# Pooled attention and a SiLU layer: a third unit in the first product, key and value sums on Pool, x sums a tile ahead

## Chip, cores and metric

The kernel runs on one core of a Trainium2 chip. Its time is the device time of one execution in microseconds; a figure for a kernel is the median of several runs. The profile names the engines: PE (TensorE: matmuls; PEld is its weight load), DVE (VectorE), ACT (ScalarE), POOL (GpSimd, which also issues the casting and adding loads) and SP (SyncE, which issues stores).

## What is computed

There are 8 batches, 8 heads, 576 queries and a head size of 64. Keys and values are averaged over groups of 8 positions, so that each query meets 72 of them. The attention result is x, 4608 tokens by 512, and goes through two matrix products with a SiLU between them.

```
k_p = k.reshape(B, H, Sp, pool, D).mean(axis=3)
v_p = v.reshape(B, H, Sp, pool, D).mean(axis=3)
attn = softmax(scale * q @ k_p^T)
x = (attn @ v_p), rearranged to 4608 x 512
h = x @ w_in              # 512 x 2048
g = h * sigmoid(h)
out = g @ w_out           # 2048 x 512
```

## The kernel before

**Tiles.** Tokens are taken 512 at a time: nine tiles, t = 0 to 8 (loop at line 801). Each tile has a first product (`up`, line 467) that fills h_T, 16 groups of 128 hidden columns, and a second one (`down_quarters`, line 639) that makes 512 output rows. The attention of batch a = t + 1 is spread over tile t. Call U the start of a tile's first product and D the start of its second.

**Order of work.** The order on each engine is written by hand. `spread` (line 413) runs beside the matmuls of a product: each matmul of a plain group, and each pair of matmuls of a unit, is a step, and each filler, a function with a step number, is issued when its step is reached. A step number therefore places work in the queue of its engine, nothing more: an engine that isn't held by a wait (Pool above all) runs ahead of PE. Fillers in `f_up` belong to the first product, those in `f_down` to the second.

**First product.** A plain group (line 534) is four matmuls of 512 columns into one PSUM bank of the tag mm (three banks), then a SiLU on ACT. A unit (lines 424 to 523) treats four groups and two halves of the tokens as a 2 x 2 block product and does it by seven products instead of eight, each of four matmuls of 256 columns. Two of its accumulators, P and Q, lie in banks of the tag at (five banks, shared with the attention), R in one of mm. ACT copies P into r_sb (line 501); DVE makes rr_sb, t_sb and two c_sb from PSUM and r_sb (lines 504, 507, 516, 519); ACT then makes SiLU from two PSUM banks and two c_sb (line 492). Units take sums of x (`unit_x_sum`, line 449, five per tile, common to all units) and sums of weights (`unit_weight_sum`, line 442, five per unit). Tiles 2 to 6 have two units (groups 4 to 11) and eight plain groups. Tiles 7 and 8 have three units, called B, C and A (groups 4 to 7, 8 to 11 and 12 to 15), and four plain groups, in an order written in `THREE` (line 794), where A2 is product 2 of unit A.

**Second product.** It uses the same seven-product scheme: 112 matmuls of 256 columns, with sums of h_T (`hidden_sum`, line 609) that DVE makes late in the first product and early in the second. PE first reads the sums 2 and 5 for hidden groups 4 to 7 of each half. The last add of a tile (line 687) empties bank Q.

**Attention.** Queries come through POOL (`load_q`, line 134, two buffers) and are transposed on DVE in four parts (`q_transpose`, line 155). Keys of batches 3 to 7 come in two loads: `load_one` (line 176) writes the first half, `load_rest` (line 182) adds the second half to it in place and so must wait until the first has landed. Then DVE adds twice: `add_halves` (line 188, 72 x 1024 fp32) and `add_rest` (line 193, 72 x 512). For keys the result is kp, one buffer, which `k_transpose` (line 213) takes through PE and ACT to kz; for values it is vp, two buffers. The raw buffers k_raw and v_raw exist once, so a new load waits until the adds on the old data are done. Then follow, in three visits per batch, scores and exponentials (line 339), denominators (359) and numerators (378), which write x (xT).

Of the kernel before, what the change touches and what calls it, by code (L numbers as in the profile page):

```python
# [29 lines left out]
BF16 = mybir.dt.bfloat16  # L30
# [6 lines left out]
def kernel(  # L37
# [9 lines left out]
    nc = tc.nc  # L47

    B, H, S, D = q.shape
    POOL = 8  # L50
    SP = S // POOL
# [75 lines left out]
    batches = {}  # L127
# [57 lines left out]
            accum_op=ALU.add,  # L185
        )

    def add_halves(raw):
        nc.vector.tensor_add(
            out=raw[:, :, : 2 * D], in0=raw[:, :, : 2 * D], in1=raw[:, :, 2 * D :]  # L190
        )

    def add_rest(dst, raw):
        nc.vector.tensor_add(
            out=dst,
            in0=raw[:, :, :D], in1=raw[:, :, D : 2 * D],
        )

    def pool_k(b, stage):
        st = batches[b]  # L200
        raw = st["k_raw"]
        if stage == 0:
            add_halves(raw)
            return
        add_rest(kp[:SP], raw)

    def pool_v(b):
        st = batches[b]
        st["vp"] = mid.tile([SP, H, D], BF16, tag="vp", name="vp")
        add_halves(st["v_raw"])  # L210
        add_rest(st["vp"], st["v_raw"])

    def k_transpose(b, parts=(0, 1)):
        st = batches[b]
# [586 lines left out]
    for t in range(NT):  # L801
        a = t + 1
        f_up, f_down = [], []
        if t == 0:
            GA = 11
            items = [(g, 0, HS) for g in range(GA)]
            items += [(g, HS, NTT - HS) for g in range(GA)]
            items += [(g, 0, NTT) for g in range(GA, KG)]
            f_up += [(1, lambda: denominators(0, part(0, 1), on_dve=True))]
            f_up += [(5, lambda: denominators(0, part(1, 1), on_dve=True))]  # L810
            f_up += [(13, lambda: numerators(0, part(0, 1)))]
            f_up += [(17, lambda: numerators(0, part(1, 1)))]
        else:
            G = lambda *gs: [(g, 0, NTT) for g in gs]
            if t == 1:
                items = (
                    G(12, 13, 14, 15) + [(0, "251")] + G(8) + [(0, "43")] + G(9)
                    + [(0, "7h6")] + G(10) + [(0, "s")] + G(11, 0, 1, 2, 3)
                )
            elif t >= B - 1:  # L820
                items = []
                for it in THREE[t - B + 1].split():
                    items += [(("BCA".index(it[0])), it[1])] if it[0] in "ABC" else G(int(it[1]))
            else:
                items = (
                    G(12, 13) + [(0, "251")] + G(14) + [(0, "43")] + G(15) + [(0, "76")]
                    + [(1, "2")] + [(0, "hs")] + [(1, "51")] + G(0) + [(1, "43")] + G(1)
                    + [(1, "7h6")] + G(2) + [(1, "s")] + G(3)
                )
            if t < B - 1:  # L830
                for n in U_X:
                    f_up.append((0, lambda n=n: unit_x_sum(t, n)))
            for n in (2, 5):
                h_at = {B - 1: 54, B: 50}.get(t, 36 if t > 1 else 45)
                f_up.append((h_at, lambda n=n: hidden_sum(n, 4, 8)))
            f_up.append((56, lambda: hidden_sum(6, 4, 8)))
            for n, k0 in ((2, 0), (5, 0), (1, 4), (1, 0)):
                f_up.append((64, lambda n=n, k0=k0: hidden_sum(n, k0, k0 + 4)))
            f_down.append((33, lambda: hidden_sum(7, 0, 8)))
            f_down.append((71 if t < B else 50, lambda: hidden_sum(6, 0, 4)))  # L840

        for n, t0, f_to, at, parts in (
            (1, 0, f_down, 48, (0, PW)), (3, 0, f_down, 52, (0, PW)),
            (4, 1, f_up, 38, (0, PW)), (7, 1, f_up, 42, (0, PW)),
            (6, 1, f_up, 60, (0, PW)),
        ):
            for i in range(*parts):
                if t == t0:
                    f_to.append((at + i, lambda n=n, i=i: weight_sum(n, i)))
        if a < B:  # L850
            q_at = [15, 16, 17, 8] if t > 1 else [24, 25, 26, 2] if t else [82, 84, 86, 88]
            if t == 0:
                for j in range(2):
                    f_up.append((44 + 8 * j, lambda j=j: slot_sums("k", j)))
                    f_up.append((72 + 8 * j, lambda j=j: select_k(1, j)))
                    f_up.append((72 + 8 * j, lambda j=j: copy_k(1, j)))
                    f_down.append((20 + 10 * j, lambda j=j: slot_sums("v", j)))
                    f_down.append((37 + 3 * j, lambda j=j: select_v(1, j, "at")))
                    f_down.append((37 + 3 * j, lambda j=j: copy_v(1, j)))
            elif t == 1:  # L860
                for j in range(2):
                    f_up.append((0, lambda j=j: slot_sums("k", j, halves=True)))
                    f_up.append((22, lambda j=j: select_k(2, j)))
                    f_up.append((23, lambda j=j: copy_k(2, j)))
                    f_down.append((8, lambda j=j: slot_sums("v", j, halves=True)))
                    f_down.append((40, lambda j=j: select_v(2, j, "at")))
                    f_down.append((41, lambda j=j: copy_v(2, j)))
            else:
                f_up.append((22, lambda: k_transpose(a)))
                f_down.append((10, lambda: pool_v(a)))  # L870
            for n in range(4):
                f_to = f_down if t and n == 3 else f_up
                f_to.append((q_at[n], lambda n=n: q_transpose(a, n % 2, n // 2)))
            if t == 0:
                f_down.append((0, lambda: load_half_2("k", 0)))
                f_down.append((0, lambda: load_q(2)))
                f_down.append((0, lambda: load_half_2("k", 1)))
                for half in range(2):
                    f_down.append((31, lambda half=half: load_half_2("v", half)))
                for y in range(2):  # L880
                    for n in U_W:
                        f_down.append((6, lambda y=y, n=n: unit_weight_sum(y, n)))
            elif a + 1 < B:
                for stage in range(2):
                    f_down.append((73 + 8 * stage, lambda stage=stage: pool_k(a + 1, stage)))
                f_up.append((0, lambda: load_one(a + 1, "k")))
                f_up.append((48 if a + 1 == B - 1 else 1, lambda: load_q(a + 1)))
                f_up.append((2, lambda: load_rest(a + 1, "k")))
                f_down.append((11, lambda: load_one(a + 1, "v")))
                f_down.append((12, lambda: load_rest(a + 1, "v")))  # L890
            f_down.append((0, attn_tables))

            if t:
                sc_at, den_at, nu_at = (1, 31, 75), (31, 56, 97), (56, 97, 101)
            else:
                sc_at, den_at, nu_at = (1, 16, 30), (16, 30, 44), (44, 55, 56)
            for n, sg in enumerate(visits):
                f_down.append((den_at[n], lambda sg=sg: denominators(a, sg)))
                f_down.append((sc_at[n], lambda sg=sg: scores(a, sg)))

            for n, sg in enumerate(visits):
                if n < 2 or not 0 < t < B - 2:
                    f_down.append((nu_at[n], lambda sg=sg: numerators(a, sg)))
                if n == 0 and 1 < t < B - 1:
                    f_down.append((nu_at[n], lambda: numerators(a - 1, visits[2])))
        if t in (B - 2, B - 1):
            for n in (4, 1, 3, 7, 6):
                f_down.append((98 if t < B - 1 else 44, lambda n=n: unit_x_sum(t + 1, n)))
        if t == B - 2:
            k_w = big.tile([128, 4, 2, 256], BF16, tag="k_raw2", name="w_sum12")  # L910
            v_w = big.tile([128, 4, 2, 256], BF16, tag="v_raw2", name="w_sum12")
            w_sum1.append([k_w[:, i] for i in range(4)] + [v_w[:, 0]])
            for i, n in enumerate(U_W):
                f_down.append((73 if i < 2 else 81, lambda n=n: unit_weight_sum(2, n)))
        moe_tables()
        up(t, f_up, items)
        if t == 0:
            down(t, f_down, [(0, 1, 2), (3,)])
        else:
            down_quarters(t, f_down, last=t == NT - 1)  # L920
# [28 lines left out]
```

The softmax here doesn't subtract the row's maximum and nothing guards it: scores larger than these inputs give would overflow.

## Time and profile before

| | |
|---|---|
| median of 4 runs | 283.62 us (283.2 to 283.7) |
| profiled execution | 283.7 us |
| its span | 281.6 us |
| PE busy | 276.1 us |
| DVE busy | 223.2 us |
| ACT busy | 184.9 us |
| POOL busy | 61.1 us |
| first product, tiles 3 to 6 | 13.14, 13.16, 13.20, 13.10 us |
| second product, tiles 3 to 5 | 15.98, 16.00, 16.00 us |
| first product, tile 7 (three units) | 12.62 us |

The span goes from the first instruction to the last; the execution's own time has 2.1 us more around it. Rows of groups give a line of the kernel, the engine and operation, out<-in, the count, then busy time and the mean duration of one in ns, then the idle time before them and what ended it. Rows of a timeline give start and duration in us; neighbouring instructions of a kind are merged, and the end of one may lie past the start of the next. Rows of stretches give start and end, length, and the busy time of each engine. In these tables the tiles' products are cut at their first matmuls.

### The profile page before, as it was taken

How to read it: one execution, taken by the hardware profiler on the slowest of the kernel's cores; microseconds unless marked ns; L12 is line 12 of the kernel's file. 1: busy time of each engine (PE TensorE's matmuls, PEld its weight loads, DVE VectorE, ACT ScalarE, POOL GpSimd, SP SyncE). 2: the span in 40 equal slices, each digit the busy share in tenths (PEclk: the TensorE clock that was granted, in tenths of full speed). 3: DMA queues.
4: the chain of work that ended last, by engine and by line, in shares of the span. 5: the costliest groups of instructions: out<-in, count | busy, mean ns of one | idle time of the engine just before them, and what ended most of it. 6: DMA issues, size and time to landing. Idle time of an engine off the chain costs nothing.

```text
span 281.6 us, 6986 instructions
## 1 busy us (share of the span) xinstructions
PE 276.1 (98%) x2823; PEld 198.0 (70%) x2823; DVE 223.2 (79%) x413; ACT 184.9 (66%) x361; POOL 61.1 (22%) x79
## 2 busy tenths in 40 slices
PE   8989999999999999999999999999999999999995
PEld 4348544456777677767888876687767878788784
DVE  4787736889977798779877996898878898966983
ACT  1677766568577876687668857794779568426800
POOL 8565216232140214021402130442200000000001
PEclk9999999999999999999999999999999999999999
DMA  7999999896759853985497539499750032004004
GB/s 210 277 256 236 209 312 178 224 187 123 144 74 211 153 121 51 196 188 123 69 197 168 107 80 173 106 153 133 115 120 1 2 84 67 2 6 127 20 4 147
DMA packets 31312, 37.70 MB, mean 134 GB/s; under 512 B 10352, under 2 KB 22256, under 8 KB 31280
## 3 DMA queue, kind: packets, MB, share of 16 engines
q0 software_dynamic: 23920, 27.03, 52.7%
q1 hardware_dynamic: 6928, 9.58, 12.5%
q10 hardware_dynamic: 432, 0.66, 0.7%
q8 instruction: 22, 0.36, 0.5%
q14 instruction: 10, 0.08, 0.1%
HBM read 36.70 MB, written 9.44 MB: 164 GB/s over the span
## 4 chain that ended last, share of the span: by engine, by line
PE 91%; DMA 3%; DVE 3%; POOL 1%; issue 1%; DVEq 0%; POOLq 0%
PE hp_ps L544 24%; PE o_psP L652 15%; PE o_psQ L652 15%; PE u_psQ L484 8%; PE u_psP L484 8%; PE o_psR L652 5%; PE sc_ps L347 4%; PE o_ps L579 3%; DMA raw<-in_v_dram 3%; PE nu_ps L391 3%; PE u_psR L484 3%; PE den_ps L365 2%; DVE xT L400 1%; DVE w_sum L630 1%; POOL q_bf L132 1%
## 5 line engine op out<-in xcount | busy, mean ns | idle before, releaser
L544 PE MATMUL hp_ps<-xT,w_in_sb 128*128 128x512 bf16 (+3 forms) x380 | 74.5, 337 | 0.1
L652 PEld LDWEIGHTS <-h_sum 128*128 128x128 bf16 x640 | 60.6, 98 | 11.9 <-issue 1.3
L550 ACT ACTIVATE h_T<-hp_ps 128x512 bf16<-128x512 f32 (+2 forms) x87 | 46.4, 541 | 18.2 <-PE hp_ps L544 16.0
L612 DVE TENSOR_TENSOR h_sum<-h_T 128x1024 bf16<-128x1024 bf16 (+1 forms) x72 | 50.5, 744 | 5.0 <-ACT h_T L550 5.0
L544 PEld LDWEIGHTS <-w_in_sb 128*128 128x128 bf16 x380 | 36.2, 98 | 21.8 <-issue 0.6
L355 ACT ACTIVATE es<-sc_ps 72x384 bf16<-72x384 f32 (+1 forms) x100 | 39.0, 469 | 9.7 <-PE sc_ps L347 9.6
L484 PEld LDWEIGHTS <-w_sum 128*128 128x128 bf16 x340 | 33.3, 98 | 7.5
L652 PEld LDWEIGHTS <-h_T 128*128 128x128 bf16 x256 | 24.1, 98 | 4.5 <-issue 0.9
L400 DVE TENSOR_TENSOR xT<-nu_ps,rec 128x384 bf16<-128x384 f32 (+1 forms) x50 | 24.0, 534 | 2.0 <-PE nu_ps L391 1.8
L374 ACT ACTIVATE lnd<-den_ps 128x384 f32<-128x384 f32 (+1 forms) x23 | 11.1, 484 | 19.6 <-PE den_ps L365 19.6
L492 ACT ACTIVATE h_T<-c_sb 128x512 bf16<-128x512 f32 x34 | 20.7, 626 | 4.4 <-DVE c_sb L516 4.2
L270 DVE TENSOR_TENSOR raw<-raw 128x384 f32<-128x384 f32 (+3 forms) x20 | 12.4, 619 | 9.7 <-DMA raw<-in_v_dram 6.9
L516 DVE TENSOR_TENSOR c_sb<-u_psP,t_sb 128x512 f32<-128x512 f32 x17 | 11.7, 690 | 8.4 <-ACT kz L224 4.2
L183 POOL DMA_DIRECT2D raw<-in_k_dram x5 | 7.1, 1429 | 50.7 <-DMA raw<-in_k_dram 50.7
L556 POOL DMA_DIRECT2D out_dram<-o_sb x2 | 1.2, 592 | 77.0 <-issue 76.2
L652 PE MATMUL o_psP<-w_out_sb,h_sum 128*128 128x256 bf16 x128 | 17.6, 273 | 0.0
L501 ACT COPY r_sb<-u_psP 128x512 f32<-128x512 f32 x17 | 9.9, 584 | 10.3 <-PE u_psP L484 9.0
L652 PE MATMUL o_psQ<-w_sum,h_sum 128*128 128x256 bf16 x128 | 16.7, 273 | 0.0
L652 PE MATMUL o_psQ<-w_out_sb,h_sum 128*128 128x256 bf16 x128 | 16.6, 273 | 0.0
L652 PE MATMUL o_psQ<-w_sum,h_T 128*128 128x256 bf16 x128 | 16.5, 273 | 0.0
L652 PE MATMUL o_psP<-w_sum,h_T 128*128 128x256 bf16 x128 | 16.5, 273 | 0.0
L504 DVE TENSOR_TENSOR rr_sb<-u_psQ,r_sb 128x512 f32<-128x512 f32 x17 | 11.8, 691 | 5.6 <-ACT r_sb L501 5.0
(83 smaller groups left out, 466.9 us busy)
## 6 DMA issues: line engine op xcount, KB each, us to landing
out_dram<-o_sb SPq DMA_DIRECT2D x128, 64.0 KB, 4.6
raw<-in_k_dram POOLq DMA_DIRECT2D x10, 576.0 KB, 9.7
raw<-in_v_dram POOLq DMA_DIRECT2D x10, 576.0 KB, 7.9
q_bf<-in_q_dram POOLq DMA_DIRECT2D x6, 576.0 KB, 12.9
w_in_sb<-in_moe_w_in_dram POOLq DMA_DIRECT2D x8, 256.0 KB, 8.4
w_out_sb<-in_moe_w_out_dram POOLq DMA_DIRECT2D x4, 512.0 KB, 13.7
raw<-in_v_dram POOLq DMA_DIRECT2D x2, 768.0 KB, 11.3
raw<-in_k_dram POOLq DMA_DIRECT2D x1, 768.0 KB, 9.5
```

The lines of the kernel that those rows point to most:

```text
L270: nc.vector.tensor_add(out=raw[..., :w], in0=raw[..., :w], in1=raw[..., w : 2 * w])
L347: nc.tensor.matmul(sc[s][:, cs], lhsT=kz[b % 2][rows, g, c, :], rhs=st["qT"][rows, g, i0:i1, :, c], start=(c == 0), stop=(c == 1),)
L355: nc.scalar.activation(es[:, s, :], sc[s], func=AF.Exp, scale=score_scale)
L400: nc.vector.tensor_mul(out=xT[:, 2 * g0 + c : 2 * (g0 + ng - 1) + c + 1 : 2, cols], in0=nu[c][:, :w].rearrange("r (g n) -> r g n", g=ng), ...
L484: nc.tensor.matmul(ps[y, bank][:, u, :], lhsT=w[:, kk, 128 * u : 128 * (u + 1)], rhs=x[:, kk, :], start=first and u == 0 and kk == 0, stop ...
L492: nc.scalar.activation(h_T[:, g : g + 2, j * NQ : (j + 1) * NQ], src, func=AF.Silu)
L504: tt(out=rr_sb, in0=ps[y, "Q"], in1=r_sb, op=ALU.add)
L516: tt(out=c_sb[0], in0=ps[y, "P"], in1=t_sb, op=ALU.add)
L544: nc.tensor.matmul(hp_ps[:, r0:r1], lhsT=w_in_sb[:, kk, g * 128 : (g + 1) * 128], rhs=xT[:, kk, x0 : x0 + r1 - r0], start=(kk == 0), stop= ...
L550: nc.scalar.activation(h_T[:, g, n0 : n0 + n], hp_ps[:, :n], func=AF.Silu)
L612: nc.vector.tensor_tensor(out=h_sum[n][:, ks, :], in0=quarter(*a, ks), in1=quarter(*b, ks), op=op)
L652: nc.tensor.matmul(ps[b][:, c, :], lhsT=left(n, kt, c), rhs=W_OUT[n][:, kt, :], start=b not in begun, stop=kt == k1 - 1, skip_group_check= ...
```

## The change

1. Tiles 3 to 6 get the third unit too: the plain groups 12 to 15 become unit A, in the order of `THREE`.
2. The adds on raw keys and values of batches 3 to 7 go from DVE to POOL (`pool_rows`). The value adds of batch a are issued at step 2 of the first product of tile a - 1, in POOL's queue behind the first key load and the query load of batch a + 1 and ahead of the second key load; the key adds of batch a + 1 at step 13 of the second product, ahead of the second value load. From tile 2 on the first value load is issued in the first product. For batch 7 the query load comes later, behind the first value load.
3. The five sums of x for tiles 3 to 6 are issued at step 98 of the second product of the tile before, not at the start of their own tile.
4. The weight sums of unit A are made in tile 1 instead of tile 6.
5. From tile 3 on, the key transpose is issued at the head of the first product instead of step 22, two of the four query transposes at steps 4 and 14 of the first product and two at steps 4 and 8 of the second (before: three and one), and the first sums of h at step 54 instead of 36.

```diff
-    def add_halves(raw):
-        nc.vector.tensor_add(
+    def pool_rows(dst, raw):
+        nc.gpsimd.tensor_add(
             out=raw[:, :, : 2 * D], in0=raw[:, :, : 2 * D], in1=raw[:, :, 2 * D :]
         )
...
+        nc.gpsimd.tensor_add(out=dst, in0=raw[:, :, :D], in1=raw[:, :, D : 2 * D])
+
+    def pool_k(b):
+        pool_rows(kp[:SP], batches[b]["k_raw"])
 
     def pool_v(b):
         st = batches[b]
         st["vp"] = mid.tile([SP, H, D], BF16, tag="vp", name="vp")
-        add_halves(st["v_raw"])
-        add_rest(st["vp"], st["v_raw"])
+        pool_rows(st["vp"], st["v_raw"])
...
-            elif t >= B - 1:
+            elif t > 2:
                 items = []
-                for it in THREE[t - B + 1].split():
+                for it in THREE[t // B].split():
...
-            if t < B - 1:
+            if t < 3:
                 for n in U_X:
                     f_up.append((0, lambda n=n: unit_x_sum(t, n)))
             for n in (2, 5):
-                h_at = {B - 1: 54, B: 50}.get(t, 36 if t > 1 else 45)
+                h_at = 50 if t == B else 54 if t > 2 else 36 if t > 1 else 45
...
-            q_at = [15, 16, 17, 8] if t > 1 else [24, 25, 26, 2] if t else [82, 84, 86, 88]
+            q_at = [4, 14, 4, 8] if t > 2 else [15, 16, 17, 8] if t > 1 else [24, 25, 26, 2] if t else [82, 84, 86, 88]
...
-                f_up.append((22, lambda: k_transpose(a)))
-                f_down.append((10, lambda: pool_v(a)))
+                f_up.append((0 if t > 2 else 22, lambda: k_transpose(a)))
+                f_up.append((2, lambda: pool_v(a)))
             for n in range(4):
-                f_to = f_down if t and n == 3 else f_up
+                f_to = f_down if t and n >= (2 if t > 2 else 3) else f_up
...
-                for stage in range(2):
-                    f_down.append((73 + 8 * stage, lambda stage=stage: pool_k(a + 1, stage)))
+                f_down.append((13, lambda: pool_k(a + 1)))
                 f_up.append((0, lambda: load_one(a + 1, "k")))
                 f_up.append((48 if a + 1 == B - 1 else 1, lambda: load_q(a + 1)))
-                f_up.append((2, lambda: load_rest(a + 1, "k")))
-                f_down.append((11, lambda: load_one(a + 1, "v")))
-                f_down.append((12, lambda: load_rest(a + 1, "v")))
+                f_up.append((3, lambda: load_rest(a + 1, "k")))
+                f_to, at = (f_up, 4) if t > 1 else (f_down, 12)
+                f_to.append((at, lambda: load_one(a + 1, "v")))
+                f_down.append((14, lambda: load_rest(a + 1, "v")))
...
-        if t in (B - 2, B - 1):
+        if 1 < t < B:
             for n in (4, 1, 3, 7, 6):
                 f_down.append((98 if t < B - 1 else 44, lambda n=n: unit_x_sum(t + 1, n)))
-        if t == B - 2:
-            k_w = big.tile([128, 4, 2, 256], BF16, tag="k_raw2", name="w_sum12")
-            v_w = big.tile([128, 4, 2, 256], BF16, tag="v_raw2", name="w_sum12")
-            w_sum1.append([k_w[:, i] for i in range(4)] + [v_w[:, 0]])
+        if t == 1:
+            def unit_weight_tiles():
...
+            f_down.append((72, unit_weight_tiles))
             for i, n in enumerate(U_W):
                 f_down.append((73 if i < 2 else 81, lambda n=n: unit_weight_sum(2, n)))
```

## The prediction

> **What bounds the kernel.** I read the page from the top: span, busy shares, chain.
>
> ```profile
> span 281.6 us, 6986 instructions
> ...
> PE 276.1 (98%) x2823; PEld 198.0 (70%) x2823; DVE 223.2 (79%) x413; ACT 184.9 (66%) x361; POOL 61.1 (22%) x79
> ...
> PE 91%; DMA 3%; DVE 3%; POOL 1%; issue 1%; DVEq 0%; POOLq 0%
> ```
>
> PE is never free: 98% busy, 91% of the chain. So time is won by PE instructions left out, and lost where PE is made to wait. The view of busy time by stretches, cut at the first matmuls of tile 3's two products and of tile 7's first product, shows both forms of the first product (columns: length, then busy time of PE, PEld, DVE, ACT, POOL):
>
> ```profile
> 111.32:124.46 13.14, 13.14 (x94) 8.75 (x92) 10.61 (x20) 9.78 (x19) 1.43 (x1) 1.00 0.98 190
> 124.46:140.44 15.98, 15.98 (x222) 12.74 (x221) 13.52 (x21) 11.69 (x24) 3.80 (x4) 1.00 0.55 105
> 228.45:241.07 12.62, 12.62 (x102) 9.79 (x101) 10.88 (x19) 9.68 (x19) 0.00 (x0) 1.00 0.27 68
> ```
>
> PE is busy for the whole of each, at clock 1.00. The third line is tile 7, which already runs three units with sums of x made a tile ahead; that is what tiles 3 to 6 are to become. Call U the start of a tile's first product, D that of its second.
>
> **PE's part.** PE's timeline in tile 7 gives the pace, from start to start:
>
> ```profile
> 229.22 1.03 PE L544 MATMUL hp_ps<-xT,w_in_sb 128*128 128x512 bf16 x4
> 230.09 0.60 PE L484 MATMUL u_psP<-xT,w_sum 128*128 128x256 bf16 x4
> 230.53 0.60 PE L484 MATMUL u_psP<-x_sum,w_in_sb 128*128 128x256 bf16 x4
> ...
> 240.97 1.04 PE L652 MATMUL o_psP<-w_out_sb,h_sum 128*128 128x256 bf16 x8
> ```
>
> Four 512-column matmuls take 0.87 us (0.217 each); four of 256 columns 0.437 (0.109 each; over 230.53 to 240.97 the pace holds). In each of tiles 3 to 6 the four plain groups 12 to 15 go (16 x 0.217 = 3.47 us) and seven products come (28 x 0.1093 = 3.06): 0.41 us saved, 1.64 over four tiles. In tile 4 the plain groups are split in two halves of 256 columns, which costs the same. Cross-check by stretches: tiles 3 to 6 take 13.14, 13.16, 13.20 and 13.10 us, tile 7 12.62. The former also hold the transpose of keys, 13.14 - (32 x 0.217 + 56 x 0.1093) = 0.08, which stays. So 13.15 - 12.70 = 0.45 each, 1.8 in all. I take the smaller, 1.64.
>
> **DVE's part.** A 0.69 us row back to back costs 0.605 from start to start. Per first product: four more such sums on PSUM (2.42); five sums of x leave (1.70), one of three query transposes leaves (0.40). Per second product: the adds of keys and values leave, sums of x and the transpose come (2.10). The rows for the adds, and the only Pool rows that are elementwise work:
>
> ```profile
> L189 DVE TENSOR_TENSOR raw<-raw 72x1024 f32<-72x1024 f32 x10 | 12.0, 1196 | 0.0
> L194 DVE TENSOR_TENSOR vp<-raw 72x512 bf16<-72x512 f32 x5 | 3.4, 687 | 0.2
> L194 DVE TENSOR_TENSOR kp<-raw 72x512 bf16<-72x512 f32 x5 | 3.4, 678 | 0.0
> masks.py:199 POOL TENSOR_SCALAR_AFFINE_SELECT shifts<-shifts 128x128 bf16<-128x128 bf16 x1 | 0.5, 480 | 0.1
> L724 POOL MEMSET shifts<- 128x328 bf16 x1 | 0.4, 443 | 0.0
> ```
>
> Two pairs leave, 2 x (1.13 + 0.61) = 3.5 us of DVE per tile. In all DVE loses about 1 us of work per tile. None of that is on the path, so I count it as zero. What hides it is PE's own work; what counts is the place where PE reads what DVE has just made. In tile 7 that is the start of the second product:
>
> ```profile
> 239.52 0.69 DVE L519 TENSOR_TENSOR c_sb<-u_psQ,t_sb 128x512 f32<-128x512 f32 x1
> 240.13 4.29 DVE L612 TENSOR_TENSOR h_sum<-h_T 128x1024 bf16<-128x1024 bf16 x7
> ```
>
> Seven sums of h follow one another from D - 0.84 (D = 240.97) to D + 3.45. PE reads the first at D, the second 0.87 later, the fourth at D + 1.75 (ready D + 1.6), the last at D + 3.5. Tile 7 loses nothing, but by under 0.2 us. In tiles 3 to 6 the scores (0.44 us) come first, at step 1, so all but the first have 0.5 to 0.9 to spare. Two query transposes follow (till D + 4.3) and PE's scores of the second visit need the first of them at D + 4.44 (128.80 - 124.36): covered, narrowly. ACT gains one 0.58 copy; its 9.7 us of 12.6 in tile 7, with gaps of 0.5 to 0.7 early on, leave room for it and for the 0.42 copy of keys. If the cover is gone, each of these becomes a PE wait of its own size.
>
> Tile 1: five weight sums of 0.35 (1.7 us) come into DVE's queue at steps 73 and 81, where the adds of keys (1.74) go: even. Their absence in tile 6 frees DVE where PE wasn't waiting: zero. The sums of x now stand in DVE's queue ahead of the last o_sb add (line 687), which ends 0.9 us later; the bank that it frees is needed only for A1, 2.6 us into the product: zero.
>
> **Pool's queue.** The trace shows no Pool add. Bounds for a pair: DVE's rows, 1.9 us; MEMSET, (443 - 100)/327 = 1.05 ns per element over the 0.1 us of a one-element memset, 1.8; AFFINE_SELECT, which also reads SBUF, (480 - 100)/128 = 3.0 ns, 3.1 + 1.6 = 4.8. I take 4.8, the row nearest in kind, and keep 1.8. The Trainium skill, GPSIMD Engine Reference, section 3.1, gives 4497 ns for 2048 fp32 elements; by it a pair would be an estimated 3.4 us. No run here shows it.
>
> Pool runs ahead of PE, so its own chain decides; all landings below are from the list of DMA issues by window. Its timeline before, around tile 3:
>
> ```profile
> 108.16 1.40 POOL L183 DMA_DIRECT2D raw<-in_v_dram  x1 [6.11 <-issue]
> 109.00 1.40 POOL L179 DMA_DIRECT2D raw<-in_k_dram  x1
> 109.82 1.32 POOL L150 DMA_DIRECT2D q_bf<-in_q_dram  x1
> 121.52 1.43 POOL L183 DMA_DIRECT2D raw<-in_k_dram  x1 [10.38 <-DMA raw<-in_k_dram]
> ```
>
> New order: first k, q, value adds, second k, first v, key adds, second v. Second k of batch 3: issued 66.4, lands 7.5 later, adds till 78.7; second v behind it at 78.7 (was 78.3), lands 10.6 later; value adds till 94.1; second k of batch 4 behind them at 94.1 (was 92.2), lands 8.4 later, adds till 107.3. The key transpose, now at the head of tile 3, needs them at 111.2: 3.9 us to spare. Next round: second v 107.3 + 9.7, adds to 121.8, second k + 8.2, adds to 134.8, needed at 139.9. A round is 27.5 us, under the 28.7 of a tile, so it doesn't fall back. With 1.8 a pair the margin is 9 us. Loads come earlier or within 2 us of before; first v goes from 101.2 to 95.5. q's slot is free from D + 4.3 of the tile before. Queued behind Pool's new waits are only loads and adds with these margins: zero.
>
> **What speaks against it.** Before, Pool writes descriptors (the eight q issues, 180.79 to 186.03) beside sums of h at 0.684 us each, as elsewhere: Pool's writing doesn't slow DVE. Pool reading SBUF beside a DVE add with both inputs in SBUF isn't in the trace. Bounds: nothing, or DVE held for the whole Pool add, 1.2 to 3.1 us for the longer one. The Trainium skill, SBUF — State Buffer, section "Who interferes with whom", says the latter: the two share a read port and whoever comes second is fully blocked. By the rule one meeting with the sums of h would end at an estimated 284.6, where the sum without it ends at 282.1; no run here shows it. I take nothing for the likeliest, since with 4.8 a pair the adds lie outside D - 0.84 to D + 3.45 in each tile (keys of batch 5: 130.0 to 134.8 with D = 123.9; values of 4: 117.0 to 121.8), while DVE's other sums have the 1 us and more that left it. With 1.8 a pair, keys of batch 5 would come near 124 to 126, inside it.
>
> **The cases.**
> - No stall: 283.70 (profiled execution: 281.6 span and 2.1 around it) - 1.64 = 282.06, 282.1; 282.0 against the median 283.62, which the profiled one exceeds by 0.08. Own range 281.8 (by 0.45 a tile) to 282.4. Chance 0.56.
> - Small stalls at D: one meeting with the short end, 1.2 less 0.5, or 0.2 a tile at the narrow places: +0.8, 282.9. Chance 0.12.
> - The gain is eaten: stalls of about 1.6: 283.7. Chance 0.10.
> - Slower: Pool's adds hold DVE inside the run of sums of h. Price 3.1 less 0.65 = 2.5 a meeting: one 284.6, two 287.1. It decides once stalls pass 1.64 + 0.57 = 2.2. For it: 27% of a tile's 28.7 us lies within reach of that run (4.3 + 3.4). Against it: Pool's chain puts the adds elsewhere at 4.8. Chance 0.18 (0.12 for one).
> - Slower, Pool late: if a pair took 9.6, keys of batch 4 would end at 121.7 and PE stand 10 us: 292 and over. Chance 0.04; no row is that slow.
> That the exchange of plain groups for units brings PE nothing is excluded by tile 7.
>
> 0.2% is 0.57 us, about what a measurement of this kernel can tell from no change. Faster 0.68, same 0.10, slower 0.22. Range 281.7 to 285.0: it leaves out two meetings, the late Pool and some tails.
>
> **What would show it.** First products of tiles 3 to 6 of 12.7 us with PE busy throughout; Pool adds of 3.1 and 1.6; kp ready before U; sums of h still 0.684 us and second products still 16.0. I am wrong if sums of h stretch or wait for Pool, if the second products grow, or if the key transpose waits.

## Result and the profile after

The changed kernel takes 0.9973 [0.9966, 0.998] of the time before: 282.5 us where the kernel before has a median of 283.31. 24 of the 47 executions of the changed kernel took 286.3 to 292.8 us and are left out of this ratio, while none of 67 of the kernel before was above 284.01. Over all 47 the median is 286.3 us, 1.1% above the kernel before: the gain of 0.3% holds for the other half alone. The profiled execution, a short one, took 282.29 us (span 280.3; before 283.7 and 281.6).

From the page of the changed kernel: span, busy shares, shares of the chain, then the groups of the sums of h and of the new Pool add.

```profile
span 280.3 us, 7086 instructions
...
PE 275.6 (98%) x2855; PEld 201.4 (72%) x2855; DVE 220.3 (79%) x409; ACT 187.6 (67%) x365; POOL 100.8 (36%) x99
...
PE 91%; DMA 3%; DVE 3%; POOL 1%; issue 1%; DVEq 0%; POOLq 0%
...
L601 DVE TENSOR_TENSOR h_sum<-h_T 128x1024 bf16<-128x1024 bf16 (+1 forms) x72 | 53.0, 787 | 1.0 <-ACT h_T L539 1.0
...
L189 POOL TENSOR_TENSOR raw<-raw 72x1024 f32<-72x1024 f32 x10 | 24.5, 2448 | 57.0 <-DMA raw<-in_v_dram 19.9
```

PE is as full as before, and the chain is the same. POOL went from 61.1 to 100.8 us busy. The 72 sums of h do the same work as before, but went from a mean of 744 ns to 787: something slows them. Their row on the page before:

```profile
L612 DVE TENSOR_TENSOR h_sum<-h_T 128x1024 bf16<-128x1024 bf16 (+1 forms) x72 | 50.5, 744 | 5.0 <-ACT h_T L550 5.0
```

The view of busy time by stretches (columns as in the prediction: PE, PEld, DVE, ACT, POOL) shows tile 3's two products and tile 4's second:

```profile
111.37:124.12 12.75, 12.75 (x106) 9.91 (x104) 11.15 (x21) 10.53 (x20) 5.90 (x4) 1.00 0.97 195
124.12:140.10 15.98, 15.98 (x222) 12.73 (x220) 12.15 (x22) 11.62 (x24) 7.49 (x5) 1.00 0.67 121
152.89:168.88 15.99, 15.99 (x223) 12.73 (x221) 13.07 (x22) 11.61 (x24) 6.68 (x4) 1.00 0.63 124
```

Lengths by tile, cut at the first matmul of each product:

| product | before | after |
|---|---|---|
| first, tiles 3 to 6 | 13.14, 13.23, 13.15, 13.15 | 12.75, 12.79, 12.75, 12.75 |
| second, tile 2 | 15.99 | **16.28** |
| second, tiles 3 to 6 | 15.98, 15.98, 15.97, 16.53 | 15.98, 15.99, 15.98, 16.53 |
| opening, up to tile 0's first product | 17.19 | 17.04 |
| all others | | within 0.1 of before |

(Both kernels are cut here at each product's first matmul. The stretches in the prediction are cut 0.1 us later; this moves up to 0.07 us between neighbours.) Tiles 3 to 6 gained 1.6 us, tile 2 gave 0.3 back. Its timeline shows why; here DVE and POOL in tile 2, then in tile 4, from the changed kernel:

```profile
90.87 0.69 DVE L496 TENSOR_TENSOR t_sb<-u_psR,rr_sb 128x512 f32<-128x512 f32 x1
91.48 2.36 DVE L601 TENSOR_TENSOR h_sum<-h_T 128x1024 bf16<-128x1024 bf16 x2
...
89.26 2.35 POOL L189 TENSOR_TENSOR raw<-raw 72x1024 f32<-72x1024 f32 x1 [7.54 <-PE u_psP L473]
91.69 1.60 POOL L192 TENSOR_TENSOR vp<-raw 72x512 bf16<-72x512 f32 x1
...
152.02 4.29 DVE L601 TENSOR_TENSOR h_sum<-h_T 128x1024 bf16<-128x1024 bf16 x7
157.84 2.23 DVE L601 TENSOR_TENSOR h_sum<-h_T 128x2048 bf16<-128x2048 bf16 x1
...
156.63 2.35 POOL L189 TENSOR_TENSOR raw<-raw 72x1024 f32<-72x1024 f32 x1 [7.39 <-DMA raw<-in_k_dram]
159.07 2.14 POOL L192 TENSOR_TENSOR kp<-raw 72x512 bf16<-72x512 f32 x1
```

Two sums of h alone take 1.28 us; beside the value adds 2.36. Behind them PE's scores of the second visit start 4.74 us after the product's first matmul (99.83 - 95.09) instead of 4.44 (99.67 - 95.23), which is the 0.30 us. The t_sb add, with one input in PSUM, takes its usual 0.69 us in the middle of Pool's add. The large sum alone takes 1.21; here it begins at 157.84, and finishes 1.1 us after Pool's first add has ended at 158.98. Pool's second add, 1.27 us alone, then takes 2.14, for it waits for that sum. So of an add on Pool and a sum on DVE with both inputs in SBUF, whichever comes second stands still until the first is done. In tile 4 this costs PE nothing, since that sum isn't due yet. But the run of seven sums before it ended at 156.31, and Pool's add began at 156.63: it missed the run by 0.3 us.

### The profile page after: what moved, and what is told of

It reads as the page before. It is cut to its first block, busy times and chain, and to the rows that moved or that the text cites. A ratio compares the mean times of both kernels' runs of the same rounds, so it can differ in the third digit from the quotient of the medians.

```text
span 280.3 us, 7086 instructions
## 1 busy us (share of the span) xinstructions
PE 275.6 (98%) x2855; PEld 201.4 (72%) x2855; DVE 220.3 (79%) x409; ACT 187.6 (67%) x365; POOL 100.8 (36%) x99
## 4 chain that ended last, share of the span: by engine, by line
PE 91%; DMA 3%; DVE 3%; POOL 1%; issue 1%; DVEq 0%; POOLq 0%
PE hp_ps L533 19%; PE o_psP L641 16%; PE o_psQ L641 15%; PE u_psP L473 10%; PE u_psQ L473 10%; PE o_psR L641 5%; PE sc_ps L336 4%; PE o_ps L568 4%; PE u_psR L473 3%; DMA raw<-in_v_dram 3%; PE nu_ps L380 3%; PE den_ps L354 2%; DVE xT L389 1%; DVE w_sum L619 1%; POOL q_bf L132 1%
## 5 line engine op out<-in xcount | busy, mean ns | idle before, releaser
L533 PE MATMUL hp_ps<-xT,w_in_sb 128*128 128x512 bf16 (+3 forms) x300 | 58.2, 337 | 0.1
L601 DVE TENSOR_TENSOR h_sum<-h_T 128x1024 bf16<-128x1024 bf16 (+1 forms) x72 | 53.0, 787 | 1.0 <-ACT h_T L539 1.0
L473 PEld LDWEIGHTS <-w_sum 128*128 128x128 bf16 x420 | 40.8, 98 | 7.7
L539 ACT ACTIVATE h_T<-hp_ps 128x512 bf16<-128x512 f32 (+2 forms) x71 | 36.4, 528 | 12.8 <-PE hp_ps L533 10.5
L189 POOL TENSOR_TENSOR raw<-raw 72x1024 f32<-72x1024 f32 x10 | 24.5, 2448 | 57.0 <-DMA raw<-in_v_dram 19.9
L533 PEld LDWEIGHTS <-w_in_sb 128*128 128x128 bf16 x300 | 28.6, 98 | 18.1 <-issue 0.6
L481 ACT ACTIVATE h_T<-c_sb 128x512 bf16<-128x512 f32 x42 | 26.1, 626 | 4.0 <-DVE c_sb L505 3.4
L496 DVE TENSOR_TENSOR t_sb<-u_psR,rr_sb 128x512 f32<-128x512 f32 x21 | 14.5, 692 | 7.2 <-PE u_psR L473 5.4
L473 PEld LDWEIGHTS <-w_in_sb 128*128 128x128 bf16 x168 | 16.4, 98 | 2.8
L493 DVE TENSOR_TENSOR rr_sb<-u_psQ,r_sb 128x512 f32<-128x512 f32 x21 | 14.3, 682 | 3.7 <-ACT r_sb L490 2.1
L505 DVE TENSOR_TENSOR c_sb<-u_psP,t_sb 128x512 f32<-128x512 f32 x21 | 14.4, 688 | 3.2 <-PE u_psP L473 0.8
```

Of the source, the lines that this page charges most:

```text
L189: nc.gpsimd.tensor_add(out=raw[:, :, : 2 * D], in0=raw[:, :, : 2 * D], in1=raw[:, :, 2 * D :])
L473: nc.tensor.matmul(ps[y, bank][:, u, :], lhsT=w[:, kk, 128 * u : 128 * (u + 1)], rhs=x[:, kk, :], start=first and u == 0 and kk == 0, stop ...
L481: nc.scalar.activation(h_T[:, g : g + 2, j * NQ : (j + 1) * NQ], src, func=AF.Silu)
L493: tt(out=rr_sb, in0=ps[y, "Q"], in1=r_sb, op=ALU.add)
L496: tt(out=t_sb, in0=ps[y, "R"], in1=rr_sb, op=ALU.subtract)
L505: tt(out=c_sb[0], in0=ps[y, "P"], in1=t_sb, op=ALU.add)
```

## Experiments

Theory: the third unit gives 0.4 us of PE per tile and nothing else matters to PE; Pool adds are harmless as long as they lie outside the sums of h that PE is about to read, and dear when they meet them. Rivals: DVE needed the relief, so that the unit without the Pool adds gives less; Pool's stores, not its reads, disturb DVE; the x sums made ahead are what saves time. Ratios are against the kernel before on the same chip.

**1. The unit without the Pool adds.** Adds back on DVE at their old steps, loads in their old order; unit, x sums ahead and weight sums as changed.

```diff
-        nc.gpsimd.tensor_add(
+        nc.vector.tensor_add(
...
-                f_up.append((2, lambda: pool_v(a)))
+                f_down.append((10, lambda: pool_v(a)))
...
-                f_down.append((13, lambda: pool_k(a + 1)))
+                for stage in range(2):
+                    f_down.append((73 + 8 * stage, lambda stage=stage: pool_k(a + 1, stage)))
```

> The changed kernel with its adds of keys and values put back on DVE, at the steps and with the order of loads that they had before; the third unit and the x sums a tile ahead stay. Theory A (the gain is only PE's arithmetic, 0.40 us in each of tiles 3 to 6; whatever is missing of 1.6 is lost where a Pool add holds back a DVE add that reads two SBUF tensors): DVE then has 10.6 + 13.5 + 2.4 = 26.5 us of work in a tile of 28.7, so there is room in total; no DVE add of hidden sums takes over 0.69 us for 1024 elements; 281.9 if nothing is late, up to 283.3 if the crowded second product costs 0.3 us a tile. Theory B (the relief of DVE is what pays, the third unit is late at the start of the second product by itself): slower than before, 284 or more.

Measured: 281.3 us, 0.9922 [0.9911, 0.9934], below the changed kernel's interval. Its page:

```profile
PE 274.2 (98%) x2855; PEld 200.8 (72%) x2855; DVE 232.8 (83%) x429; ACT 187.4 (67%) x365; POOL 61.1 (22%) x79
...
L607 DVE TENSOR_TENSOR h_sum<-h_T 128x1024 bf16<-128x1024 bf16 (+1 forms) x72 | 49.8, 743 | 1.0 <-ACT h_T L545 1.0
```

DVE does 9.6 us more than before (223.2) and sums of h are at their old mean. First products of tiles 3 to 6 are 12.75 to 12.79, every second product is as before, tile 2's too (15.98), and from 60 to 240 us PE waits for no other engine. The relief of DVE wasn't needed. Of the 2.3 us between the spans (279.3 and 281.6), 1.6 lies in tiles 3 to 6 and 0.7 in the opening before tile 0 (16.50 against 17.19 us), which the change doesn't touch (see run 10).

**2. The Pool adds without the unit**: the kernel before with `pool_rows` and the new order of loads.

```diff
-        nc.vector.tensor_add(
+        nc.gpsimd.tensor_add(
...
-                f_down.append((10, lambda: pool_v(a)))
+                f_up.append((2, lambda: pool_v(a)))
...
-                f_down.append((12, lambda: load_rest(a + 1, "v")))
+                f_down.append((14, lambda: load_rest(a + 1, "v")))
```

> The kernel before with nothing but the adds of keys and values of batches 3 to 7 on Pool and the changed order of the loads; two units and own x sums in tiles 3 to 6 as before. Theory A: nothing to gain, since PE is busy throughout: 283.3 if no Pool add meets the sums of h, and up to 2 us more a meeting (284 to 288), with sums of h of 1.0 to 3 us in the trace where they meet. Theory B: DVE's relief pays, 282.5 or less.

Measured: 290.99 us, 1.026 [1.0237, 1.0284]. Second products of tiles 2, 4 and 5 grew to 17.49, 17.27 and 18.38, tile 4's first to 15.31. In the second products sums of h were met (the two in tile 2 took 3.76 us). In tile 4's first product it was the x sums, in their old place (timeline of DVE, POOL and PE; five x sums alone take 1.76 us):

```profile
142.39 4.98 DVE L440 TENSOR_TENSOR x_sum<-xT 128x512 bf16<-128x512 bf16 x5
...
142.56 2.45 POOL L189 TENSOR_TENSOR raw<-raw 72x1024 f32<-72x1024 f32 x1 [5.96 <-DMA raw<-in_v_dram]
145.09 1.33 POOL L192 TENSOR_TENSOR vp<-raw 72x512 bf16<-72x512 f32 x1
...
148.03 0.60 PE L473 MATMUL u_psQ<-x_sum,w_in_sb 128*128 128x256 bf16 x4 [1.92 <-DVE rr_sb L493]
```

The sums end after both adds, rr_sb stands behind them in DVE's queue, and PE waits 1.92 us. So this part of the change by itself, with the x sums in their old place, costs 2.6%; all five executions took 289.8 to 292.0 us.

**3. Pool writes but doesn't read.** The changed kernel with each add replaced by a memset of the same rows.

```diff
-        nc.gpsimd.tensor_add(
-            out=raw[:, :, : 2 * D], in0=raw[:, :, : 2 * D], in1=raw[:, :, 2 * D :]
-        )
-        nc.gpsimd.tensor_add(out=dst, in0=raw[:, :, :D], in1=raw[:, :, D : 2 * D])
+        nc.gpsimd.memset(raw[:, :, : 2 * D], 0.5)
+        nc.gpsimd.memset(dst, 0.5)
```

> The changed kernel with each Pool add replaced by a memset of the same destination, so that Pool writes at the same places and behind the same waits but reads nothing; the adds on keys and values of batches 3 to 7 are left out. Theory A: no DVE add is held, all sums of h of 1024 elements at 0.69 us, tile 2 loses its 0.3 us wait, 281.7 with under 1 us between runs. Theory B: as the changed kernel, 282.5, with the same spread between runs.

Measured: 281.73 us, 0.9937 [0.9922, 0.9951]. Sums of h again have a mean of 743 ns, and tile 2's second product is 15.98. In tile 2 the memsets lie right beside the two sums (DVE and POOL), and these take 1.28 us as alone:

```profile
91.76 1.28 DVE L599 TENSOR_TENSOR h_sum<-h_T 128x1024 bf16<-128x1024 bf16 x2
...
91.57 0.94 POOL L189 MEMSET raw<- 72x1024 f32 x1 [8.42 <-DMA raw<-in_v_dram]
92.46 0.52 POOL L190 MEMSET vp<- 72x512 bf16 x1
```

So Pool's place in the queue and its stores are harmless. The memsets are shorter than the adds (1.5 us a pair instead of 3.6), but a sum isn't held for their length either. What holds DVE is an add that reads; runs 4 and 5 keep the reading and move it.

**4. Adds held clear of the run of sums.** A memset on DVE, and one on Pool that follows it, hold the value adds to their first product and the key adds until the large sum of h is issued. Tile 2's first sums of h go to step 54, the second value load to step 36.

```diff
+    def hold(name):
+        gate = singles.tile([SP, 1], FP32, name=name)
+        nc.vector.memset(gate, 0.0)
+        nc.gpsimd.memset(gate, 0.0)
...
+                f_up.append((2, lambda: hold(f"gate_v{t}")))
                 f_up.append((2, lambda: pool_v(a)))
...
-                f_down.append((13, lambda: pool_k(a + 1)))
+                f_down.append((34, lambda: hold(f"gate_k{t}")))
+                f_down.append((35, lambda: pool_k(a + 1)))
```

> The changed kernel with Pool's adds held, by a one-element memset on DVE and one on Pool behind it, to places where DVE has no add with two SBUF inputs: value adds until the x sums are done, key adds until the sum of h for product 7 is done; in tile 2 the first sums of h move from step 36 to 54. Theory A: 281.7 to 281.9 with under 1 us between runs, 0.5 us better than the changed kernel; only the short sum of h at step 71 may be held. Theory B: as the changed kernel, 282.5, or slower by what the holding costs.

Measured: 282.25 us (281.74 to 284.48, 12 executions), 0.9963 [0.9947, 0.998]: not the 281.3 of run 1. In its profile tile 2 is whole again (15.99), and one product alone lost, tile 5's second, 16.52. There Pool was late behind the eight query pieces of batch 7, and its adds met the last sum of h (DVE and POOL):

```profile
191.40 3.16 DVE L601 TENSOR_TENSOR h_sum<-h_T 128x1024 bf16<-128x1024 bf16 x1
...
191.64 2.36 POOL L189 TENSOR_TENSOR raw<-raw 72x1024 f32<-72x1024 f32 x1
194.08 1.60 POOL L192 TENSOR_TENSOR kp<-raw 72x512 bf16<-72x512 f32 x1
```

A sum of 0.68 took 3.16, o_sb behind it came late, and PE waited 0.38 us. Yet none of the 12 executions is among the long ones of the changed kernel (286.3 and more).

**5. The meeting forced.** The changed kernel with the value adds of tiles 3 to 6 held until step 53 of the first product, where the run of sums begins; the first value load follows them there.

```diff
+                if t > 2:
+                    f_up.append((53, lambda: hold(f"gate_v{t}")))
-                f_up.append((2, lambda: pool_v(a)))
+                f_up.append((53 if t > 2 else 2, lambda: pool_v(a)))
```

> The changed kernel with the value adds of batches 4 to 7 held, by the one-element memsets, until DVE begins the run of sums of h before the second product of tiles 3 to 6, and the first value load behind them. Theory A (a Pool add that reads holds DVE's next add with two SBUF inputs for its whole length): the second sum of h waits 2.35 us and the third 1.27 more; PE reads them at margins of 0.5 to 0.9, so it loses about 1.5 and then 1.6 us in each of the four tiles, 12 us in all: 292 to 295, and sums of h of up to 3 us in the trace. Rival (the two share the port, or the loss comes from loads that land late): sums of h grow by less than half and the kernel stays under 285.

Measured: 307.86 us, 1.086 [1.0842, 1.0878], more than expected: second products of 23.27, 23.87, 22.86 and 19.41 in tiles 3 to 6. Timeline of DVE, POOL and PE in tile 3:

```profile
123.66 10.93 DVE L601 TENSOR_TENSOR h_sum<-h_T 128x1024 bf16<-128x1024 bf16 x6
...
123.28 2.66 POOL L189 TENSOR_TENSOR raw<-raw 72x1024 f32<-72x1024 f32 x1
126.02 1.60 POOL L192 TENSOR_TENSOR vp<-raw 72x512 bf16<-72x512 f32 x1
...
128.80 2.36 POOL L189 TENSOR_TENSOR raw<-raw 72x1024 f32<-72x1024 f32 x1
131.24 1.60 POOL L192 TENSOR_TENSOR kp<-raw 72x512 bf16<-72x512 f32 x1
...
131.77 1.89 PE L641 MATMUL o_psP<-w_out_sb,h_sum 128*128 128x256 bf16 x8 [4.17 <-DVE h_sum L601]
133.45 1.91 PE L641 MATMUL o_psQ<-w_out_sb,h_sum 128*128 128x256 bf16 x8
```

Six sums, 3.7 us alone, took 10.93: all four adds fell into them, for the run, held up by the value adds, was still going when the key adds began (128.80, against 129.22 in the changed kernel). And after a wait of 4.17 us PE needs 1.9 us for eight matmuls that take 1.04 elsewhere. The stretch behind the wait has a granted clock (third number from the end) of 0.57:

```profile
132.00:136.00 4.00, 4.00 (x36) 2.37 (x34) 3.86 (x6) 0.75 (x2) 2.69 (x4) 0.57 0.13 34
```

**6. x sums in their own tile**, the rest as changed.

```diff
-            if t < 3:
+            if t < B - 1:
                 for n in U_X:
...
-        if 1 < t < B:
+        if t in (B - 2, B - 1):
```

> The changed kernel with the x sums of tiles 3 to 6 back at the start of their own first product; third unit and Pool adds stay. Theory A: the x sums then stand from U + 0.9 to U + 2.6, where the value adds come in tiles 4 and 5 (U + 2.8 and U + 1.1 in the changed kernel), and are held as in the kernel with Pool adds alone, where the five took 4.98 us instead of 1.75: 284 to 287, with PE waiting for rr_sb or x_sum in one or two of these tiles. Rival (moving the x sums only moves DVE work): 282.5, as the changed kernel.

Measured: 290.13 us, 1.0238 [1.0186, 1.0291]; both expectations were too low. But the x sums were a small part of the cause: they took 1.76 us in tiles 3 and 4 and 2.37 in tile 5, where rr_sb behind them came late, PE waited 0.49 us and the first product took 13.40 instead of 12.79. The key adds had met the run of sums of h, in tile 4 (below) and tile 5; these second products were 17.75 and 19.52.

```profile
151.69 6.45 DVE L601 TENSOR_TENSOR h_sum<-h_T 128x1024 bf16<-128x1024 bf16 x7
...
155.05 2.54 POOL L189 TENSOR_TENSOR raw<-raw 72x1024 f32<-72x1024 f32 x1 [6.55 <-DMA raw<-in_k_dram]
```

What released Pool is a load, not an x sum: the add came 2.5 us after the start of the second product (152.56), and in the first profile of the changed kernel 3.7 after it. Whether the old place of the x sums brings this on isn't shown, since run 12 has the same without it. All four executions here (288.0 to 292.2 us) and all five of run 2 are long, against half of the changed kernel's: that is suggestive, no more.

**7. Run 1 with the x sums in their own tile** (run 1 and run 6's edit).

> The kernel with the third unit and the adds on DVE, but the x sums of tiles 3 to 6 at the start of their own first product. Theory A: without Pool adds nothing holds the x sums, and A4 needs the first of them only 2.2 us after U, so PE waits for nothing: 281.3 to 281.6, the same as with x sums ahead. Rival (the unit order needs the x sums ahead): 0.3 to 0.9 us more in each of four tiles, 282.5 to 285.

Measured: 281.81 us, 0.9949 [0.9935, 0.9963]; first products 12.80 to 12.83 against 12.75 to 12.79. Sums of x made ahead are worth 0.05 us a tile, 0.2 in all.

**8. Run 1 with the unit from tile 2 on** (with tile 2's query transposes, sums of h and x sums placed as in tile 3).

```diff
-            elif t > 2:
+            elif t > 1:
                 items = []
```

> The kernel with the third unit and the adds on DVE, with tile 2 too in the form of tiles 3 to 6: third unit, x sums a tile ahead, key transpose at the head, its query transposes and first sums of h at their steps. Theory A: one more tile saves 0.40 us of PE: 280.9 against 281.3. Rival (tile 1's second product, where DVE also makes five weight sums and the last slot sums, has no room for the x sums): no gain or a loss of up to 1 us, 281.3 to 282.3.

Measured: 281.17 us, 0.9928 [0.9915, 0.994]. Tile 2's first product is 12.75 (13.15 before): the same 0.40 once more in the trace, too little to tell from run 1 by times.

**9. Run 4 with batch 7's queries loaded at step 1**, so that Pool isn't late in tile 5.

```diff
-                f_up.append((48 if a + 1 == B - 1 else 1, lambda: load_q(a + 1)))
+                f_up.append((1, lambda: load_q(a + 1)))
```

> The changed kernel with its adds held as before, and the query load of batch 7 issued at step 1 of tile 5's first product like the others, so that its eight parts no longer stand ahead of the key adds of batch 7 in Pool's queue (in the held kernel they put these adds 4 us late, at 191.64, where the sum of h at step 71 took 3.16 us and PE waited). Theory A: no Pool add then meets a DVE add with two SBUF inputs, none of which takes over 1.22 us, and tile 5's second product is back at 15.98: 281.3 to 281.7, as with the adds on DVE, which would show that Pool adds cost nothing in themselves. Rival (Pool adds cost something wherever they lie): 282.2, as the held kernel.

Measured: 283.6 us, 1.0012 [0.9998, 1.0026]: the expectation failed. The query pieces now stand before the value adds of batch 6, which came late, at 178.89, and met the start of the run of sums in tile 5 (5.37 us instead of 4.29); its second product is 16.69. In tile 1 the key adds of batch 3 met the sum at step 71 (2.04 us instead of 0.68), 16.80 instead of 16.17. In runs 4 and 9, each place that was cleared sent adds to another sum. Again none of the 12 executions was long (282.6 to 284.8 us). So it is shown for tiles 2 to 4, where no sum that PE needs was met, that Pool adds cost nothing (15.99, 15.98, 15.98), and not for a whole kernel.

**10. The kernel before, unedited.**

> The kernel before, unchanged, for a second trace of its opening. In the trace that the prediction used, tile 0's second product took 12.10 us; in those of the kernels since, 11.46 to 12.30, though none of them changes anything in tile 0. If that length varies from run to run, this trace gives another one between 11.4 and 12.3, with the same 29.1 us for each of tiles 2 to 5; if it belongs to the kernel, 12.1 again.

Measured: 283.18 us. The lengths that this expectation and that of run 12 give for tile 0 are misread: they run from the start of a row near 40 us, not from the product's first matmul. Cut there, tile 0's second product takes 18.28 us in both profiles of this kernel, and 18.3 in all others but run 12 (18.54) and run 3 (18.90). What does vary is the opening before tile 0's first product: 16.64 us here, 17.19 in the first profile, 16.50 to 17.19 over all runs, with no order by edit. Everything behind it agrees to 0.02. So the opening's length is none of the change's doing.

**11 and 12. The changed kernel, unedited, twice more.** The question was whether its narrow places hold from one execution to the next.

> The changed kernel itself, profiled a second time; nothing is edited. In its first profile the key adds on Pool began 0.3 to 0.4 us behind the end of the run of sums of h in tile 4 (156.63 against 156.3), and the value adds of tile 2 met two sums of h. Theory, a narrow order: the loads' landing times differ a little from execution to execution, so the adds on Pool fall differently against the sums of h; where the key adds begin inside the run, that sum stretches past 2 us and its second product grows by 1.5 us or more; where they begin behind it, the second products of tiles 3 to 5 are again 15.98 and the whole is about 282. Rival, a fixed order: the adds fall as in the first profile to within 0.1 us, tile 2's second product is again 16.28 and the others 15.98.

> The changed kernel itself, profiled a third time, beside the second look on the same chip. Narrow order: at least one of the three profiles differs from the others by a meeting, with a sum of h stretched past 2 us in the tile whose second product grew, and products without a meeting unchanged to 0.05 us. Fixed order: the lengths of all products agree to 0.05 us in all three, but for tile 0's second one, which varied in the other runs (11.46 to 12.30).

Measured: 283.06 and 291.71 us. The order isn't fixed. In the first, the key adds of batch 3 met the sum at step 71 of tile 1 (DVE and POOL), and PE waited 0.9 us behind it; second products of tiles 1 and 2 were 17.23 and 16.21, those of tiles 3 to 5 whole.

```profile
75.41 2.47 DVE L601 TENSOR_TENSOR h_sum<-h_T 128x1024 bf16<-128x1024 bf16 x1
...
74.98 2.36 POOL L189 TENSOR_TENSOR raw<-raw 72x1024 f32<-72x1024 f32 x1 [2.93 <-DMA raw<-in_k_dram]
```

In the second, tiles 2, 4 and 5 lost: second products of 18.33, 19.41 and 19.38. Against the first profile of the changed kernel these are 2.05, 3.42 and 3.40 us, which with 0.43 in tile 1 and 0.25 in tile 2's first product give 9.5, the difference of the spans (289.8 and 280.3; tile 0's 0.3 more and the opening's 0.3 less cancel). Timeline of DVE, POOL and PE in tiles 2, 4 and 5:

```profile
92.14 4.40 DVE L601 TENSOR_TENSOR h_sum<-h_T 128x1024 bf16<-128x1024 bf16 x2
154.73 6.45 DVE L601 TENSOR_TENSOR h_sum<-h_T 128x1024 bf16<-128x1024 bf16 x7
186.92 8.05 DVE L601 TENSOR_TENSOR h_sum<-h_T 128x1024 bf16<-128x1024 bf16 x7
...
91.98 2.34 POOL L189 TENSOR_TENSOR raw<-raw 72x1024 f32<-72x1024 f32 x1 [8.29 <-DMA raw<-in_v_dram]
158.20 2.43 POOL L189 TENSOR_TENSOR raw<-raw 72x1024 f32<-72x1024 f32 x1 [6.50 <-DMA raw<-in_k_dram]
189.78 2.36 POOL L189 TENSOR_TENSOR raw<-raw 72x1024 f32<-72x1024 f32 x1
...
161.63 0.72 PE L336 MATMUL sc_ps<-qT,kz 32*72 32x192 bf16 x16 [1.52 <-DVE qT L158]
162.28 3.58 PE L641 MATMUL o_psR<-w_sum,h_sum 128*128 128x256 bf16 x16
192.75 1.05 PE L641 MATMUL o_psQ<-w_out_sb,h_sum 128*128 128x256 bf16 x8 [1.63 <-DVE h_sum L601]
195.41 0.73 PE L336 MATMUL sc_ps<-qT,kz 32*72 32x192 bf16 x16 [1.33 <-DVE qT L158]
```

How it came about can be followed back. The second key load of batch 3 was issued at 67.98 instead of 65.98, when the first one had landed. The adds on it then met sums on DVE (3.58 us instead of 2.36), the second value load went out at 80.67 instead of 78.70, and the value adds came at 91.98 instead of 89.26, where both Pool adds fell into two sums of h. That made PE late: tile 4's second product began at 155.60 instead of 152.89, 2.7 us; Pool, which follows its loads, was late by 1.6 (158.20 instead of 156.63). So its key adds came earlier against PE: in tiles 3 and 4 they lie 5.1 and 3.7 us behind the start of the second product in the first profile, 4.7 and 2.6 in this one, the latter inside the run. Here the meetings delayed PE by more than Pool, and that makes the next one likelier; tile 5's stood at 7.1 and now at 2.0.

## Why the prediction held, and where it didn't

- **PE's part** (0.41 us in each of tiles 3 to 6, 1.64 in all): right. 0.39, 0.44, 0.40 and 0.40, and 0.40 for tile 2 in run 8. The cross-check's 0.45 was too high: these products stand 0.13 above tile 7's, where it allowed 0.08 for the key transpose.
- **DVE's part costs nothing, x sums ahead nothing, weight sums in tile 1 even**: right for PE. The closest thing to a cost, the x sums, is 0.05 us a tile to the good. The prediction didn't ask whether DVE's relief was needed; run 1 shows that it wasn't.
- **Pool's queue**: the pair was mis-sized. I took 4.8 us from AFFINE_SELECT; it is 2.35 + 1.27 = 3.6. Keys were ready in good time (107.45, first needed at 111.4). The Trainium skill's figure (GPSIMD Engine Reference, section 3.1) gave an estimated 3.4, nearer than my row. The shorter pair lets the key adds of batch 5 begin 5.1 us behind the start of the second product instead of my 6.1.
- **"I take nothing for the likeliest"** is the step that failed, in its reason if not in the sign. Pool adds do hold DVE's sums for their whole length, and sums hold Pool. The adds weren't clear of them in each tile: tile 2's value adds cost 0.29 us in the first profile. "A round is 27.5 us, under the 28.7 of a tile" was read as safety. The round was 27.4 (129.22 to 156.63), and this is what brought the key adds 1.4 us nearer to the run of sums from tile 3 to tile 4. And tile 2 was overlooked: "outside D - 0.84 to D + 3.45 in each tile" fits tiles whose sums of h start at step 54. Tile 2 keeps step 36, where the kernel before makes two of them at 91.44, 3.8 us ahead of its second product; the prediction's own times for the value adds of batch 3, 89.3 to 94.1, cover that. "Sums of h still 0.684" failed.
- **The rival's price**, 2.5 us a meeting, was too low for the run of seven: 3.4 in tiles 4 and 5 of run 12 and 3.5 in tile 5 of run 6, though 1.8 in tile 4 of run 6; a meeting with the two sums of tile 2 cost 0.3 to 2.4. Its two meetings at 287.1 are 291.7 in run 12, with a third in tile 2, above the range. So is the median of all executions, 286.3; the rival had a chance of 0.18 and came true in about half of them. The rule of the Trainium skill (SBUF — State Buffer, "Who interferes with whom") that a DVE instruction with two SBUF inputs and a Pool instruction that reads SBUF shut each other out agrees with 2.23 for 1.21 us on DVE and 2.14 for 1.27 on Pool, and with run 3. It deserved more than the weight I gave it.
- So 282.1 forecast and 282.5 measured agree through one right term and one meeting in the part that the ratio compares; by the mechanism, the forecast and its rival both happen, in different executions. One long execution was profiled, and for it the sum closes. That all 24 long ones are such meetings isn't shown one by one. But none of the 22 executions of runs 1, 3, 7 and 8, where Pool adds nothing, took over 282.9 us, and none of the 24 of runs 4 and 9, which hold the adds, over 284.8: the long ones come with Pool adds that aren't held.

**Open**: what moves a load's landing by 2 us from one execution to the next; what sets the opening's 16.50 to 17.19; and whether the opening is also why run 1 gains 0.6 us more by its median than its tiles 3 to 6 explain.

## What to carry to other kernels

Look for the part of a change that makes the gain and ask whether the other parts are needed: here the third unit with all adds left on DVE takes 0.9922 [0.9911, 0.9934], while the Pool adds without the unit cost 2.6%, and with it half of the executions take 3 to 10 us more than the kernel before. Before elementwise work goes to Pool, list DVE's instructions with two SBUF inputs around the place where it will land, and count that place as uncertain by as much as its loads are. A queue that follows its loads and a queue that follows PE drift against each other; a margin of 0.3 us in one profile isn't a margin.

## What the hardware did that I had not expected

A wait of PE can cost twice its length. In run 12 the wait of 1.52 us in tile 4 was followed by 16 matmuls in 3.58 us instead of 1.92, at half the clock; the view by stretches, granted clock third from the end:

```profile
158.00:160.00 2.00, 2.00 (x21) 1.50 (x19) 2.00 (x2) 1.85 (x5) 1.80 (x1) 1.00 0.52 175
...
161.00:163.00 2.00, 1.37 (x20) 0.91 (x21) 2.00 (x5) 0.94 (x3) 2.00 (x2) 0.82 0.04 8
163.00:165.00 2.00, 2.00 (x11) 1.42 (x10) 0.64 (x1) 0.96 (x3) 1.51 (x2) 0.50 0.18 19
165.00:168.00 3.00, 3.00 (x53) 2.26 (x51) 1.28 (x3) 0.72 (x2) 0.00 (x0) 0.88 1.01 143
```

With a clock of 1.00 or 0.50, these shares make an estimated 0.7 + 2 + 0.7 = 3.4 us at half clock, from 162.3 to 165.7. The same came behind a wait of 1.62 us in tile 5 of run 6 (0.50 from 192 to 194). It doesn't follow each wait: in tile 5 of run 12, waits of 1.63 and 1.33 us left the clock at 1.00, as did 1.92 us in run 2, while 4.17 us in run 5 brought it to 0.57. The Trainium skill (TensorE: Matmul & The Clock Gate, Part 1, "What's actually happening") says that the clock is halved after an idle window of about 3.4 us which runs freely; half the clock and the 3.4 us agree with run 12, but here less than half that time of idling was enough. The moment alone doesn't decide it either: if windows of 3.4 us follow one another from 162.3 on, one runs by estimate from 189.5 to 192.9, and the wait of 1.63 us (191.1 to 192.7) lies inside it as well. What decides is open.
